# Block-causal attention with a gated convolutional unit: V rows of two tokens, masks by a minimum, products of 128x128, a searched order

## The chip, the cores and the metric

The kernel runs on one core of one Trainium2 chip. The metric is the device time of one execution in microseconds. Three runs of the kernel before have a median of 193.28 us (193.21 to 194.22). A profiled execution of it stands in the profile below, and all durations come from that one.

## What is computed

Eight batches of eight heads, 576 tokens, head width 64, all in float32. First attention whose mask is causal in blocks of 64 tokens, then a gated linear unit whose gate is a causal convolution of 5 taps along the tokens:

```python
scores = scale * np.matmul(q, k.transpose(0, 1, 3, 2))
mask = block_i >= block_j                      # blocks of 64 tokens
attn = softmax(np.where(mask, scores, -1e9))
x = np.matmul(attn, v)                         # (8, 8, 576, 64) -> (8, 576, 512)
gate = sigmoid(sum(conv_w[k] * xp[:, k:k + S, :] for k in range(5)))
out = (gate * (x @ w_val)) @ w_out             # (8, 576, 512)
```

## The kernel before, in words

The unit of work is a pair of heads; there are 32 pairs, four to a batch. The kernel is laid out as *steps*. Each step belongs to one engine and issues a handful of instructions there. A step's kind is a letter:

- **T** (33 steps, 16 products each, the first pair's in two of 8): `transposes` (L171) turns the fp16 casts of K and Q by identity products into PSUM; `evict_k` (L192, line L449) and `evict_q` (L458) copy them into the tile `kq`. **U** (8 steps): the same for the last 64 tokens of a batch (`evict_tail`, L480).
- **S** (three per pair): `scores` (L236), products of 64 rows; the two heads of a pair run in the two halves of the array. `exps` (L523) takes the exponential on ScalarE, 1024 columns a step, into the tile `pt`.
- masks: where a 128-row block of keys reaches beyond what a block of queries may see, the second half of its rows has to be zero. `zeros` (L280, line L542) writes zeros over rows 64 to 127 of two strips of `pt` per head, twice a pair, and `keep_last` (L274, line L530) copies one strip's rows 64 to 127 into `pd`. Each of these steps is on VectorE or GpSimd.
- **P** (one per pair, 30 products of 128x128 with 65 columns): `products` (L292) multiplies `pt` with the values `ve`, whose 65th column is one, so that the row sums come along. `sums` (L573) and `normal` (L583) divide on VectorE.
- **X** (10 products): `xt_steps` (L594) turns the result into `xt` (`evict_x`, L606). **G** (20 products of 64x64): `gate`, the convolution as products with diagonal matrices; `tanh` on ScalarE (L629).
- **V** (64 steps, 8 products of 128x64 with 288 columns): `val` multiplies with `w_val`, the two halves of the tokens side by side in the two column halves of the array; `gated` (L651) multiplies by the gate on VectorE into `gv`.
- **O** (19 steps, 16 products of 64x128 with 512 columns; the last tile in two steps of 256 columns): `out_tile` multiplies with `w_out`, `evict_out` (L674 on ScalarE, L676 on VectorE) copies 1024 columns to `ob`, and `store` (L684) sends them out.

All products go through one helper, so their line is L255. TensorE's shape of array differs by kind: T, U, S, X, O are 64x128, G is 64x64, V is 128x64, P is 128x128.

What sets the order: the table `ORDER` gives TensorE's steps, one letter each. `CHOICE` gives the engine of each step that could run on several. A planner (`plan`) walks through all steps with a table of costs and delays and puts every step at the place in its engine's instruction stream where it would start first; the instructions are then issued in that order, and on the chip each engine works its stream in order, with semaphores between them. Loads are steps of the SP queue in the order that `queue` lists. Where the planner sees TensorE without work before 60 us, it puts *fillers* into TensorE's stream: products of a zero tile `nought` with 128 columns, which keep the array busy.

Loads: K and Q of a pair are 256 KB each in runs of 1024 bytes (512 KB for two pairs from pair 8 on), through a ring of three buffers of two pairs. V comes in runs of 256 bytes, one token of one head to a partition row (`load_head` L138 for the first two batches, `load_v` L128 afterwards, 256 KB for 128 tokens of all eight heads), through a ring of five buffers. VectorE, GpSimd or ScalarE casts each into fp16 (L416).

Of the kernel before, what the change touches and what calls it, by code (L numbers as in the profile page):

```python
# [9 lines left out]
SUM_MAX = 60000.0  # L10

# [19 lines left out]
FROM, BUSY, FILL, FULL, NOUGHT = 1050, 9500.0, 60000.0, 4700, (108, 55)  # L31


WEIGH = {"PE": 0, "DVE": 83, "ACT": 69, "POOL": 127, "SP": 0}

ORDER = (
    "TTSUSSTSSSTPSSTcXSSSSPPXGPXTXUGVSSVGTGVSVSSVPSVTVPSSXTSVXSSSPGGXPUTGXTSVVGSSVVVS"
    "SVVVSTTPSSPSOXSPSXGXSTTGGSUPSSOXSPSSVVGTTVVSSSVVVVXSTTPSUPXSGGSXPSSOSXOSGGTSVVSS"
    "VVVSUTPPTSOSSVVVSXTPSSOXXGGSSOTSPPSSOXUGGTSVVXTSVVVVSSTPPSSOXSPXGGSXVVVSSTOTUVVS"
    "SSPPGGSTVVSXSVVVSSXPPSTOSSOSTOXXGGGSSTVVVVVVSSSPPPXSGGVVPXXOXGGGVVVVVVVVOOOfOO")  # L40

CHOICE = (
    "DDDADAPPPPDDDPDDDDDPAPDDDDPPPDDADPDADPPDDAAPADPDDDDPDPPDAAADDPPDDPPDADDDPDPPDAAD"
    "PPPADPPDDPPDDDDDPPPDPPPDDAAPPPPADDDDPPPPDPDADDDPDDPPDDPPPPADDPPDDPPPDDADDDDDDPPD"
    "DPDPDDPPDDDDPPDPDAADPPPDAADADPDPDPDDDDPPPPDPPAADDDPDPDDDDDDDAPPAAPDPDDADADPPDPPD"
    "DADPPPPDPDADDPPPAPPDDDPPPADPDDPDPPDDDPDDDDPPDDADPDDDDPPDDDPPDDPPDDDDDPDPPADPPPPA"
    "AAPAAPDPPDDDDPDDDDPPDADDDDDPPDDPPPPAPDADDPPDAAA")


class Step:  # L50


    def __init__(self, kind, key, engines, emit, needs, mode, banks, size, upper):
        self.kind, self.key, self.engines, self.emit = kind, key, engines, emit
        self.needs, self.mode, self.banks = list(needs), mode, banks
        self.size, self.upper = size, upper
# [6 lines left out]
class Planner:  # L63
# [6 lines left out]
    def add(self, kind, key, engines, emit, needs=(), mode=None, banks=0, size=None, upper=False):  # L70
# [33 lines left out]
    def plan(self):  # L104
        self.rank()
        free = dict(BEGIN)
        upper = {e: False for e in ENGINES}
        bank_free = [0.0] * 7 + [BUSY]
        mode, dma = None, 0.0
        lands = [0.0] * LANES  # L110
# [33 lines left out]
        def parts(s):  # L144
            rate = s.size[1]
            return s.size[0] / (256 if rate < 250 else 1024 if 300 < rate < 320 else 2048)
# [83 lines left out]
def kernel(  # L230
# [482 lines left out]
    def holds(s, *users):  # L713
        for u in users:
            u.held = s
# [429 lines left out]
```

## Time and profile before

| what | value |
|---|---|
| median of three runs | 193.28 us |
| the profiled execution, its own time | 193.37 us |
| its span, first to last instruction | 191.4 us |
| mean granted TensorE clock | 0.990 |
| instructions: matmul, VectorE, ScalarE, GpSimd | 3898, 335, 183, 161 |
| DMA packets, bytes | 64183, 41.02 MB |

The profile is one execution. Its span is about 2 us shorter than the execution's time, which holds what lies around the instructions. An engine's busy time is the time in which one of its instructions runs. Matmuls are pipelined: the record of one is as long as its passage through the array, several overlap, and the ends are modelled; so the price of a step is read from start to start, not from a mean duration. In a timeline row "x48" is a run of 48 like instructions, and the bracket holds the engine's idle time just before and what ended it. PEld is TensorE's load of the stationary operand, which runs ahead of the products.

### The profile page before, as it was taken

The page shows a single profiled execution, that of the slowest core. Times are in us where ns is not written, and L with a number is a line of the kernel's source. Part 1 is how long each engine was busy: PE and PEld are TensorE (multiplying, and loading weights), DVE is VectorE, ACT ScalarE, POOL GpSimd, SP SyncE. Part 2 cuts the span into 40 slices and gives each one's busy share as a digit, 9 for nine tenths or more (in the row PEclk, how much of TensorE's full clock was granted, in tenths as well). Part 3 has the DMA queues.
Part 4 walks back from the last instruction along what each step waited for, and adds up shares of the span by engine and source line. Part 5 has one row for each costly group of instructions (what it writes and reads, how often), then busy time and mean ns, then how long its engine had stood idle before and what let it go on. Part 6 is the DMA issues. An engine that isn't in the chain of part 4 may idle for free.

```text
span 191.4 us, 9072 instructions
## 1 busy us (share of the span) xinstructions
PE 176.8 (92%) x3898; PEld 130.3 (68%) x3898; DVE 137.6 (72%) x335; ACT 144.1 (75%) x183; POOL 69.4 (36%) x161
## 2 busy tenths in 40 slices
PE   7978999788999989999999999999999999999940
PEld 7766876566676747686686666777688568878430
DVE  5468775685978869897989756888977786876020
ACT  3587999497788969799789889688979877743430
POOL 5224451463674615535523546142716001100000
PEclk9999999999999999999999999999999999999996
DMA  5999999799869999969999799999981062004291
GB/s 152 264 284 306 216 235 340 190 272 198 255 154 263 242 295 262 255 157 322 333 225 270 190 317 288 238 279 281 270 268 47 37 207 92 3 3 113 93 305 56
DMA packets 64183, 41.02 MB, mean 214 GB/s; under 512 B 39301, under 2 KB 58757, under 8 KB 64138
## 3 DMA queue, kind: packets, MB, share of 16 engines
q1 hardware_dynamic: 63562, 39.87, 77.3%
q8 instruction: 32, 0.52, 1.2%
q10 hardware_dynamic: 576, 0.52, 0.9%
q14 instruction: 13, 0.11, 0.2%
HBM read 30.42 MB, written 9.44 MB: 208 GB/s over the span
## 4 chain that ended last, share of the span: by engine, by line
PE 65%; DMA 15%; DVE 9%; ACT 2%; issue 2%; SPq 2%; POOL 0%; ACTq 0%; DVEq 0%; POOLq 0%
PE ps L255 59%; DMA qraw<-in_q_dram 10%; PE ps L441 3%; DMA kraw<-in_k_dram 3%; PE ps L594 3%; DMA tail<-in_q_dram 2%; DVE gv L651 2%; DVE kq L449 1%; DVE w_out L416 1%; ACT kq L458 1%; DVE xn L583 1%; DVE qc L416 1%; SPq L386 1%; DVE kq L458 1%; DVE pd L530 1%
## 5 line engine op out<-in xcount | busy, mean ns | idle before, releaser
L523 ACT ACTIVATE pt<-ps 128x1024 f16<-128x1024 f32 x96 | 94.2, 1025 | 17.3 <-PE ps L255 13.8
L255 PE MATMUL ps<-xt,w_val 128*64 128x288 f16 x512 | 36.3, 288 | 0.0
L255 PE MATMUL ps<-kq 64*128 64x64 f16 (+4 forms) x448 | 33.2, 260 | 1.8 <-DVE kq L480 0.9
L255 PE MATMUL ps<-ve,pt 128*128 128x65 f16 x896 | 33.0, 193 | 1.1 <-issue 0.8
L255 PE MATMUL ps<-w_out,gv 64*128 64x512 f16 (+1 forms) x304 | 33.7, 365 | 0.0
L255 PEld LDWEIGHTS <-pt 128*128 128x128 f16 x896 | 30.1, 97 | 4.0 <-issue 2.1
L651 DVE SCALAR_TENSOR_TENSOR gv<-th,ps 128x288 f16<-128x288 f32 x64 | 27.2, 450 | 6.3 <-PE ps L255 5.3
L255 PEld LDWEIGHTS <-w_val 128*64 128x64 f16 x512 | 27.0, 110 | 5.1 <-issue 2.9
L583 DVE TENSOR_TENSOR xn<-ps,rinv 128x640 f16<-128x640 f32 x32 | 26.4, 824 | 1.1
L255 PEld LDWEIGHTS <-kq 64*128 64x128 f16 x448 | 16.0, 94 | 14.8 <-issue 5.6
L255 PE MATMUL ps<-xt,diag 64*64 64x288 f16 x640 | 23.4, 285 | 0.0
L255 PEld LDWEIGHTS <-gv 64*128 64x128 f16 x304 | 13.8, 94 | 13.2 <-issue 0.2
L629 ACT ACTIVATE th<-ps 128x576 f32<-128x576 f32 x32 | 20.1, 660 | 1.9 <-PE ps L255 1.7
L542 POOL MEMSET pt<- 64x256 f16 x41 | 13.2, 323 | 21.0 <-ACT pt L523 15.5
L255 PEld LDWEIGHTS <-diag 64*64 64x64 f16 x640 | 17.1, 106 | 2.5 <-issue 1.0
L416 POOL CAST qc<-qraw 128x512 f16<-128x512 f32 x22 | 13.6, 629 | 12.6 <-DMA qraw<-in_q_dram 12.1
L416 POOL CAST kc<-kraw 128x512 f16<-128x512 f32 x22 | 13.5, 630 | 12.7 <-DMA kraw<-in_k_dram 10.7
L449 DVE COPY kq<-ps 128x512 f16<-128x512 f16 x19 | 13.1, 690 | 6.9 <-PE ps L441 6.4
L676 DVE TENSOR_SCALAR ob<-ps 128x1024 f32<-128x1024 f32 (+1 forms) x12 | 13.1, 1090 | 3.9 <-PE ps L255 2.3
L255 PE MATMUL ps<-nought 128*128 128x128 f16 x132 | 11.8, 250 | 1.7 <-POOL nought L343 1.0
L674 ACT ACTIVATE ob<-ps 128x1024 f32<-128x1024 f32 (+1 forms) x9 | 8.0, 885 | 6.7 <-PE ps L255 6.7
L573 DVE RECIPROCAL rinv<-ps 128x10 f32<-128x10 f32 x32 | 6.9, 216 | 8.0 <-PE ps L255 7.7
(67 smaller groups left out, 207.4 us busy)
## 6 DMA issues: line engine op xcount, KB each, us to landing
kraw<-in_k_dram SPq DMA_DIRECT2D x12, 512.0 KB, 5.2
qraw<-in_q_dram SPq DMA_DIRECT2D x12, 512.0 KB, 6.5
vraw<-in_v_dram SPq DMA_DIRECT2D x24, 256.0 KB, 6.4
out_dram<-ob SPq DMA_DIRECT2D x11, 512.0 KB, 4.0
kraw<-in_k_dram SPq DMA_DIRECT2D x8, 256.0 KB, 4.3
vraw<-in_v_dram SPq DMA_DIRECT2D x16, 128.0 KB, 5.2
qraw<-in_q_dram SPq DMA_DIRECT2D x7, 256.0 KB, 5.3
out_dram<-ob SPq DMA_DIRECT2D x4, 384.0 KB, 5.7
```

Of the source, the lines that this page charges most:

```text
L255: nc.tensor.matmul(out=out, lhsT=lhsT, rhs=rhs, start=start, stop=stop, skip_group_check=True)
L416: copier(s.engine)(out=out, in_=in_)
L441: nc.tensor.transpose(out=o, in_=c16[name][rows, t, :, :], identity=ident16[rows, rows])
L449: copier(s.engine)(out=kqs[:, p % NT, K0:K0 + 512].rearrange("p (r s t) -> p r s t", r=2, t=4), in_=ps16[:, i:i + 2, 256:512].rearrange("p ...
L523: nc.scalar.activation(out=heads(p)[:, :, 512 * c:512 * c + 512], in_=ps[:, i:i + 2, :], func=AF.Exp, bias=0.0, scale=0.125)
L542: setter(s.engine).memset(seg[:, :, :, 0:64], 0.0)
L573: nc.vector.reciprocal(out=rinv[:, p, :, :].rearrange("p e (c x) -> p e c x", x=1), in_=o[:, :, :, 64:65])
L583: nc.vector.tensor_tensor(out=xns[p % NX][:, :, :, :].rearrange("p c e d -> p e c d"), in0=o[:, :, :, 0:64], in1=ri.to_broadcast([128, 2, ...
L629: nc.scalar.activation(out=ths[at % NTH][:, 0:n, :, :].rearrange("p n r x -> p (n r) x"), in_=ps[:, i:i + 2 * n, 0:HALF], func=AF.Tanh, bi ...
L651: nc.vector.scalar_tensor_tensor(out=gv[:, 2 * g + r, s0:s0 + HALF], in0=ths[at % NTH][:, n, r, :], scalar=1.0, in1=ps[:, va.group[0], 0:H ...
L674: nc.scalar.activation(out=o, in_=x, func=AF.Copy, bias=0.0, scale=0.5)
L676: nc.vector.tensor_scalar(out=o, in0=x, scalar1=0.5, scalar2=None, op0=ALU.mult)
```

## The change

Seven edits go together.

- **V in rows of two tokens.** A partition row now holds two neighbouring tokens of a head, so a run is 512 bytes. `load_v` fetches 256 tokens of four heads in 256 KB, `load_head` as before 128 KB. The cast into `ve` becomes four (or two times two) pieces of 64 partitions (`spread`). Since key rows are now ordered by pairs of tokens, the masked rows are 32 to 63 and 96 to 127 of a 128-row block; the writes of K into `kq`, the last 64 keys and the duplicate of them follow the same order.
- **Masks.** On VectorE `zeros` and `keep_last` are a minimum over all 128 partitions with a per-partition number, 0 or 65504 (`keep`); on GpSimd they are two instructions of 32 partitions each. Eight small memsets fill `keep` at the start.
- **V as products of 128x128.** A step is 4 products of 288 columns; its left operand is the 128 columns of a group of channels or, for the second half of the tokens, the same with the 64-wide halves exchanged, for which `w_val` gets a copy of 64 columns per group.
- **O as products of 128x128.** A tile is two steps of 4 products of 512 columns, each with one bank and an eviction of 512 columns of its own; later tiles are stored in halves.
- **Loads of one pair.** K and Q are always loaded for one pair, 256 KB, through a ring of six; the table `LOADS` sets the order of all loads.
- **The planner's numbers**: delays between engines, a price for each block of 128 products on TensorE, DMA delays; and with them new tables `ORDER`, `LOADS` and `CHOICE`. TensorE's table has 137 neighbours of different array shape where there were 129.
- **Fillers** have 512 columns, are priced 430 ns before 4.7 us and 215 ns after, and stop at 25 us. There are 33 of them, 17 ahead of the first transposition; before there were 132, 30 of them ahead of it.

At the start of the SP queue, before; `kraw`, `qraw` and `vraw` are landing buffers by number; the first pair's K is ahead of these rows, its Q goes through ScalarE's queue, and the first row is the tail of K:

```order
L339 DMA tail320_96<-in_k_dram 64x1x256 x2
L333 DMA kraw0_77<-in_k_dram 128x2x256
L333 DMA qraw0_80<-in_q_dram 128x2x256
L406 DMA vtail320_100<-in_v_dram 64x8x64
L397 DMA vraw0_83<-in_v_dram 128x4x64 x2
L736 DMA conv_nat_65<-in_moe_conv_w_dram 5x512
L333 DMA kraw1_78<-in_k_dram 128x2x256
```

The same place now:

```order
L366 DMA tail320_100<-in_k_dram 64x1x256 x2
L362 DMA qraw2_85<-in_q_dram 128x2x256
L362 DMA qraw1_84<-in_q_dram 128x2x256
L362 DMA kraw1_78<-in_k_dram 128x2x256
L362 DMA kraw2_79<-in_k_dram 128x2x256
L793 DMA conv_nat_65<-in_moe_conv_w_dram 5x512
L423 DMA vraw0_89<-in_v_dram 128x2x128
L362 DMA kraw3_80<-in_k_dram 128x2x256
```

K and Q of the second and third pair have moved ahead of the first V, and V's rows are 128 elements long where they were 64.

On VectorE, around the copy of the convolution's weights `convT`, before; `kc`, `qc`, `ve` are fp16 casts, `pt` and `pd` the masked exponentials, `xt` the transposed result:

```order
L416 CAST ve0_104<-vraw1_84 128x8x64
L530 COPY pd1_112<-pt1_108 64x128
L542 MEMSET pt1_108 64x2x2x32
L449 COPY kq0_106<-ps_133 128x512
L416 COPY kq0_106<-kq0_106 128x64
L739 COPY convT_66<-ps_133 128x20
L606 COPY xt0_118<-ps_133 128x2x5x64
```

The same stretch now:

```order
L497 COPY kq0_109<-ps_136 128x512
L455 COPY kq0_109<-kq0_109 128x2x32
L455 CAST kc163_95<-kraw3_80 128x2x4x64
L796 COPY convT_66<-ps_136 128x20
L600 TENSOR_SCALAR pt0_110<-pt0_110,keep0_134 128x2x2x64 x2
L438 CAST ve0_107<-vraw0_89 64x4x64 x2
L455 CAST qc160_96<-qraw4_87 128x2x4x64
L488 COPY kq0_109<-ps_136 128x512
```

A pair's two masks are now one `TENSOR_SCALAR` each on 128 rows (before, a `COPY` and a `MEMSET` on 64), V's cast is in pieces of 64 rows, and more casts and copies of K and Q for later pairs stand ahead of the first `xt`, which is further back.

The diff, cut to its core:

```diff
-    "PE": {"PE": 0, "DVE": 265, "ACT": 250, "POOL": 240, "SP": 60},
-    "DVE": {"PE": 53, "DVE": 35, "ACT": 45, "POOL": 105, "SP": 27},
-    "ACT": {"PE": 53, "DVE": 40, "ACT": 20, "POOL": 115, "SP": 25},
-    "POOL": {"PE": 52, "DVE": 40, "ACT": 45, "POOL": 60, "SP": 30},
+    "PE": {"PE": 0, "DVE": 105, "ACT": 90, "POOL": 240, "SP": 60},
+    "DVE": {"PE": 228, "DVE": 35, "ACT": 45, "POOL": 105, "SP": 27},
+    "ACT": {"PE": 228, "DVE": 40, "ACT": 20, "POOL": 115, "SP": 25},
+    "POOL": {"PE": 228, "DVE": 40, "ACT": 45, "POOL": 60, "SP": 30},
...
+PRODUCTS = {"T": 16, "U": 8, "S": 14 / 3, "P": 30, "X": 10, "G": 20, "V": 4, "O": 4, "c": 4, "f": 1}
+BLOCK, EARLIER, BUSY_L, FREE_L = 128, 95, 4400.0, 2700.0
...
-SETUP, SEEN, LANES, SLOTS, SINGLE = 1000, 1400, 8, 2048, 8
-FROM, BUSY, FILL, FULL, NOUGHT = 1050, 9500.0, 60000.0, 4700, (108, 55)
...
+SETUP, SEEN, LANES, SLOTS, SLOW, STORED = 1000, 1700, 8, 2048, 1.05, 700
+BEFORE = (0.0, 0.0, 3950.0, 4400.0, 5900.0, 5900.0, 6100.0, 6300.0)
+FROM, FILL, FULL, NOUGHT = 1050, 25000.0, 4700, (430, 215)
...
-    "TTSUSSTSSSTPSSTcXSSSSPPXGPXTXUGVSSVGTGVSVSSVPSVTVPSSXTSVXSSSPGGXPUTGXTSVVGSSVVVS"
+    "TTUSSSTTScSSSSTSTPSSSXPGPXPSXGXUGTSVSVSTGSSVSVPTSVVSXSPVGSXSTPVSPXUGGSXTSVVSSTVV"
...
+    7, 1, 0, 6, 5, 3, 10, 8, 11, 4, 23, 2, 22, 16, 9, 18, 13, 14, 12, 17, 33, 28, 21,
...
-    w_val_sb = ring(1, [128, 4, 512], fp16, "w_val")[0]
+    w_val_sb = ring(1, [128, 4, 4, 192], fp16, "w_val")[0]
...
-    NRAW, NVR, NC, NT, NPT, NX, NXT, NTH, NOB = 3, 5, 4, 8, 4, 3, 3, 8, 4
+    NRAW, NVR, NC, NT, NPT, NX, NXT, NTH, NOB = 6, 3, 4, 8, 4, 3, 3, 7, 4
-    raws = {n: ring(NRAW, [128, 4, 4, 64], fp32, n + "raw") for n in ("k", "q")}
+    raws = {n: ring(NRAW, [128, 2, 4, 64], fp32, n + "raw") for n in ("k", "q")}
-    vraws = ring(NVR, [128, 8, 64], fp32, "vraw")
+    vraws = ring(NVR, [128, 8, 128], fp32, "vraw")
...
-    def load_v(b, c):
-        t = vraws[(4 * b + c) % NVR]
+                    lambda _: load_runs(nc.sync, src, t, p), 262144, RUN[1024],
+                    before(p - NRAW, "c" + name), 500)
+    def load_v(p, c):
+        b, j = divmod(p, PPB)
+        t = vraws[p // 2 % NVR][:, c:8:2, :]
         def emit(_):
-            nc.sync.dma_start(out=t[:, :, :],
-                              in_=v[b, :, 128 * c:128 * c + 128, :].rearrange("h p d -> p h d"))
-        n = 4 * b + c - NVR
-        return load(PPB * b - 3.5, emit, 262144, RUN[256], [chunks[n]] if n >= 0 else [], 620)
+            nc.sync.dma_start(out=t, in_=v[b, 2 * j:2 * j + 4, 256 * c:256 * c + 256, :].rearrange(
+                "h (p u) d -> p h (u d)", u=2))
...
-        t = vraws[p % NVR][:, 4 * e:4 * e + 4, :]
+        t = vraw(p)[:, 2 * e:2 * e + 2, :]
         def emit(_):
             nc.sync.dma_start(out=t, in_=v[b, 2 * j + e, 0:512, :].rearrange(
-                "(c p) d -> p c d", p=128))
-        n = p - NVR
-        return load(p - 3.5, emit, 131072, RUN[256], [chunks[n]] if n >= 0 else [], 520)
+                "(c p u) d -> p c (u d)", p=128, u=2))
...
+        def emit(s):
+            for out, in_ in todo:
+                copier(s.engine)(out=out, in_=in_)
+        return add("", key, engines, emit, needs, upper={"POOL": on, "DVE": on})
...
     def keep_last(p):
         def emit(s):
-            copier(s.engine)(
-                out=pds[p % NPT][64:128, 0:128].rearrange("p (e x) -> p e x", e=2),
-                in_=heads(p)[64:128, :, 960:1024])
+            to = pds[p % NPT][:, 0:128].rearrange("p (e x) -> p e x", e=2)
+            if s.engine == "POOL":
+                for x in (32, 96):
+                    nc.gpsimd.tensor_copy(out=to[x:x + 32], in_=heads(p)[x:x + 32, :, 960:1024])
+            else:
+                nc.vector.tensor_scalar(out=to, in0=heads(p)[:, :, 960:1024],
+                                        scalar1=keep[:, 0:1], scalar2=None, op0=ALU.min)
         return emit
     def zeros(p, first):
         def emit(s):
             if first:
-                seg = heads(p)[64:128, :, 0:1024].rearrange("p e (s x) -> p e s x", x=512)
+                at, step = 0, 512
             else:
-                seg = heads(p)[64:128, :, 960:1344].rearrange("p e (s x) -> p e s x", x=192)
-            setter(s.engine).memset(seg[:, :, :, 0:64], 0.0)
+                at, step = 960, 192
+            if s.engine == "POOL":
+                seg = halves(p)[:, :, at // 2:at // 2 + step].rearrange("p e (s x) -> p e s x", s=2)
+                for x in (32, 96):
+                    nc.gpsimd.memset(seg[x:x + 32, :, :, 0:32], 0)
+            else:
+                seg = heads(p)[:, :, at:at + 2 * step].rearrange("p e (s x) -> p e s x", s=2)
+                seg = seg[:, :, :, 0:64]
+                nc.vector.tensor_scalar(out=seg, in0=seg, scalar1=keep[:, 1:2], scalar2=None,
+                                        op0=ALU.min)
         return emit
...
     def val(b, g, r):
         def emit(s):
-            n0 = 128 * g + 64 * r
+            s0 = PAD + HALF * r
             for fc in range(4):
-                for c in range(2):
-                    s0 = PAD + HALF * c
-                    mm(out=ps[64 * c:64 * c + 64, s.group[0], 0:HALF],
-                       lhsT=w_val_sb[:, fc, n0:n0 + 64], rhs=xts[b % NXT][:, fc, s0:s0 + HALF],
-                       start=(fc == 0), stop=(fc == 3))
+                mm(out=ps[:, s.group[0], 0:HALF], lhsT=w_val_sb[:, fc, g, 64 * r:64 * r + 128],
+                   rhs=xts[b % NXT][:, fc, s0:s0 + HALF], start=(fc == 0), stop=(fc == 3))
...
+    def out_tile(i, es):
+        def emit(s):
+            for n, e in enumerate(es):
+                for g in range(4):
+                    mm(out=ps[:, s.group[0] + n, :], lhsT=gv[:, g, e, 128 * i:128 * i + 128],
+                       rhs=w_out_sb[:, 2 * g + e, :], start=(g == 0), stop=(g == 3))
...
+        "mask": memsets(0, {"DVE": 1100}, [(keep[x:x + 32, n:n + 1], (0.0, BIG)[(n + x // 32) % 2])
+                                           for x in (0, 32, 64, 96) for n in range(2)]),
...
-                o = add("O", p, {"PE": 870 if last else 1727}, out_tile(i, cols),
-                        need + lo + ([sf] if last else []), "A", 2)
+            done = []
+            for e in range(2):
+                o = add("O", p, {"PE": 870}, out_tile(i, (e,)),
+                        [pairs[x]["gv"][e] for _, _, c in parts for x in range(PPB * c, PPB * c + 4)]
+                        + lo + ([sf] if last else []), "C", 1)
...
+                    done.append(add("", p, {"ACT": 600, "DVE": 690},
+                                    evict_out(n, o, (e,), slice(0, 512)), [o] + old))
+                    holds(o, done[-1])
...
+                mid = (lo_ + hi_) // 2
+                for x, x0, x1 in (("ACT", lo_, mid), ("SP", mid, hi_)):
+                    stores[n].append(add("", p, {x: 440}, store(n, c, x0, x1, (e,)), evs,
+                                         size=((x1 - x0) * 2048, RUN[0])))
...
-                    mm(out=ps[:, s.group[0], 0:128], lhsT=nought[:, :], rhs=nought[:, :])
+                    mm(out=ps[:, s.group[0], :].rearrange("p (o x) -> p o x", o=4), lhsT=nought[:, :],
+                       rhs=nought[:, :].rearrange("p (o x) -> p o x", o=1).to_broadcast([128, 4, 128]))
```

More of the change, by code (lines that the diff above doesn't have):

```diff
@@ L106, in plan @@
         free = dict(BEGIN)
-        upper = {e: False for e in ENGINES}
-        bank_free = [0.0] * 7 + [BUSY]
+        upper = {e: 0 for e in ENGINES}
+        bank_free = [0.0] * 8
         mode, dma = None, 0.0
-        lands = [0.0] * LANES
+        count, edge, seen = 0.0, EARLIER, -1e9
+        lands = list(BEFORE)
         sent = []
@@ L904 @@
                      for c in range(UNIT) if HALF * c < x1 and HALF * c + HALF > x0]
-            need = [s for _, _, c in parts for x in range(PPB * c, PPB * c + 4)
-                    for s in pairs[x]["gv"]]
             old = [s for s in stores[n - NOB]] if n >= NOB else batches[0]["lent"].get(n, [])
@@ L948, in queue @@
                 yield from weights[2:4]
-        for p in range(8, NP, 2):
+        for p in range(8, NP):
             b = p // PPB
@@ L954, in queue @@
             if p % PPB == 0:
-                yield from (batches[b]["lv"], *batches[b]["lc"])
-    last = None
-    for s in queue():
+                yield batches[b]["lv"]
+            yield from pairs[p].get("lv", [])
+    last, listed = None, list(queue())
+    assert sorted(LOADS) == list(range(len(listed)))
+    for n in LOADS:
+        s = listed[n]
         s.load = True
```

259 lines of the change are left out of this document (141 added, 118 removed), and 7 rows, old and new, of the table LOADS.

## The prediction

> **What bounds the kernel now.** I read the page first: the engines, TensorE's busy tenths, and the shares of the chain that ended last.
>
> ```profile
> PE 176.8 (92%) x3898; PEld 130.3 (68%) x3898; DVE 137.6 (72%) x335; ACT 144.1 (75%) x183; POOL 69.4 (36%) x161
> PE   7978999788999989999999999999999999999940
> PE 65%; DMA 15%; DVE 9%; ACT 2%; issue 2%; SPq 2%; POOL 0%; ACTq 0%; DVEq 0%; POOLq 0%
> ```
>
> TensorE is the chain for two thirds of the span, with DMA behind it; its tenths dip only in the first 17 slices (4.8 us each) and at the end. A busy TensorE need not be at its peak, so I next took a stretch of its timeline in which nothing waits, where one step's start to the next one's is its price.
>
> ```profile
> 157.47 0.28 PE L441 MATMUL ps<-ident,kc 64*128 64x64 f16 x8
> ...
> 157.82 3.13 PE L255 MATMUL ps<-xt,w_val 128*64 128x288 f16 x48
> 160.89 0.86 PE L255 MATMUL ps<-kq 64*128 64x128 f16 x14
> 161.68 0.60 PE L255 MATMUL ps<-ve,pt 128*128 128x65 f16 x14
> ...
> 164.52 0.29 PE L594 MATMUL ps<-perm,xn 64*128 64x64 f16 x8
> ...
> 164.67 0.38 PE L255 MATMUL ps<-kq 64*128 64x128 f16 x6
> 164.99 1.42 PE L255 MATMUL ps<-xt,diag 64*64 64x288 f16 x40
> 166.34 1.17 PE L255 MATMUL ps<-xt,w_val 128*64 128x288 f16 x16
> ...
> 170.73 2.04 PE L255 MATMUL ps<-xt,diag 64*64 64x288 f16 x60
> 172.70 4.11 PE L255 MATMUL ps<-xt,w_val 128*64 128x288 f16 x64
> 176.74 5.35 PE L255 MATMUL ps<-w_out,gv 64*128 64x512 f16 x48
> 182.03 0.19 PE L255 MATMUL ps<-ones,allr 128*1 128x1 f32 x2
> 182.15 1.92 PE L255 MATMUL ps<-w_out,gv 64*128 64x256 f16 x32
> ```
>
> Two G and what follows take 166.34 - 164.99 = 1.35 us, three take 172.70 - 170.73 = 1.97: a G is 0.62, and 0.1 is left for the change of array shape behind it. Eight V take 4.04, six 3.07: a V is 0.49. Three O take 5.29, so 1.73 each. With 0.1 taken off for each change of shape, three P (161.68 to 164.52) are 0.91 each, a pair's S (160.89 to 161.68) 0.69, T 0.25, X 0.15. A pair is then 0.25 + 0.69 + 0.91 + 0.15 + 0.62 + 2 x 0.49 = 3.60 us, 32 pairs 115.2. Eighteen tiles of O are 31.1; the U steps and small ones I put at 1.4, an estimate at half a T each. Sum 147.7. 129 changes of shape at 0.1 add 12.9: **160.6 us** of work that no wait explains.
>
> TensorE's stream runs from 1.01 (below) to 182.15 + 1.92 = 184.07, so 183.1 us. The remaining 22.5 are fillers and waits.
>
> ```profile
> L255 PE MATMUL ps<-nought 128*128 128x128 f16 x132 | 11.8, 250 | 1.7 <-POOL nought L343 1.0
> ...
> 1.01 3.38 PE L255 MATMUL ps<-nought 128*128 128x128 f16 x30 [1.01 <-POOL nought L343]
> 4.42 0.40 PE L441 MATMUL ps<-ident,kc 64*128 64x64 f16 x8
> ...
> 5.72 1.28 PE L255 MATMUL ps<-nought 128*128 128x128 f16 x12
> 6.93 0.39 PE L255 MATMUL ps<-kq 64*128 64x512 f16 x2
> ...
> 7.37 1.12 PE L255 MATMUL ps<-nought 128*128 128x128 f16 x17
> 8.42 0.64 PE L255 MATMUL ps<-kq 64*128 64x448 f16 x12
> ```
>
> Fillers take 11.8; so **10.7 us are waits**. The load rows of TensorE show the long ones:
>
> ```profile
> 35.02 0.17 PEld L441 LDWEIGHTS <-kc 64*128 64x128 f16 x8 [1.09 <-POOL kc L416]
> 35.67 0.17 PEld L441 LDWEIGHTS <-qc 64*128 64x128 f16 x8 [0.48 <-DVE qc L416]
> ...
> 39.23 0.17 PEld L441 LDWEIGHTS <-kc 64*128 64x128 f16 x7 [0.78 <-issue]
> ...
> 45.63 0.24 PEld L255 LDWEIGHTS <-pt 128*128 128x128 f16 x6 [0.94 <-issue]
> 68.87 0.42 PEld L255 LDWEIGHTS <-kq 64*128 64x128 f16 x12 [1.04 <-DVE kq L480]
> ```
>
> Two are casts behind late K and Q. The one at 45.63 falls in the middle of a P, whose operands are all there, with "issue" beside it: TensorE had no instructions. 16 KB of them come in at a time, 32 times:
>
> ```profile
> q8 instruction: 32, 0.52, 1.2%
> ```
>
> **The change, part by part.** *V and O as 128x128.* 64 V steps of 4 products with 288 columns replace 8 products that ran two at a time: 0.49 before, 4 x 0.12 = 0.48 now, by the same columns. O: 4 products of 512 columns twice, against eight pairs of 512: 1.73 again. TensorE gains nothing here; it issues 256 + 160 products fewer. The changes of shape go from 129 to 137: +0.8.
>
> *Instructions.* 3898 becomes about 3380 products with fewer fillers, so some 28 blocks instead of 32. The wait of 0.94 goes where a dense stretch no longer meets a block's edge; I count 0.9, bounds 0 and 2. The Trainium skill, "Runtime: NRT & Kernel Launch", section Instruction fetch mechanics, says that crossing a block is mostly hidden because the engine dispatches more slowly than blocks come in. By that the saving would be 0 and the sum 0.9 higher. The row at 45.63 does not agree with it: 0.94 us without an instruction in the middle of a step.
>
> *Fillers.* A 128-column filler costs 3.38 / 30, some 0.107 us, at the start and 1.05 / 17 = 0.06 from about 6.6 us on, when the clock had risen. One of 512 columns costs four times that: 0.43 cold, 0.22 to 0.24 warm. Seventeen stand ahead of the first transposition. If the clock rises at 6.6 again, 13 run cold (5.6 us) and 4 warm (0.9): the first transposition comes at 7.5 instead of 4.42. That is 3.1 us of late start, though more of K and Q will have landed by then. The other 16 are 3.6. Together 10.1 against 11.8: -1.7. Bounds: all 17 cold, 8.3 us (+0.8); a rise at 4.5 us, -1.2.
>
> *Loads.* V in runs of 512 bytes:
>
> ```profile
> kraw<-in_k_dram SPq DMA_DIRECT2D x8, 256.0 KB, 4.3
> vraw<-in_v_dram SPq DMA_DIRECT2D x24, 256.0 KB, 6.4
> ```
>
> The same 256 KB lands in 4.3 us in runs of 1024 bytes and in 6.4 in runs of 256. With 512 it lies between; I take 5.4. That brings the first pairs' K and Q forward, which moreover now stand ahead of V in the queue, and TensorE starts 3 us later. The SP queue issues some 26 loads more at about 0.45 us, off the path. So of the 10.7 us of waits the casts behind late loads (1.09 + 0.48 + 0.78) and the small ones before 25 us (about 3) go.
>
> *VectorE.*
>
> ```profile
> L542 DVE MEMSET pt<- 64x128 uint32 x23 | 3.7, 165 | 1.8 <-ACT pt L523 1.3
> L530 DVE COPY pd<-pt 64x128 f16<-64x128 f16 x15 | 3.5, 232 | 2.3 <-ACT pt L523 2.0
> L449 DVE COPY kq<-ps 128x512 f16<-128x512 f16 x19 | 13.1, 690 | 6.9 <-PE ps L441 6.4
> L676 DVE TENSOR_SCALAR ob<-ps 128x1024 f32<-128x1024 f32 x10 | 12.2, 1223 | 2.5 <-PE ps L255 0.9 <-ACT pt L523 0.7 <-issue 0.7
> L676 DVE TENSOR_SCALAR ob<-ps 128x256 f32<-128x256 f32 x2 | 0.8, 425 | 1.4 <-PE ps L255 1.4
> ...
> 10.35 0.21 DVE L416 COPY kq<-kq 128x64 f16<-128x64 f16 x1
> ...
> 17.43 0.29 POOL L530 COPY pd<-pt 64x128 f16<-64x128 f16 x1
> ...
> 17.43 0.58 DVE L416 COPY kq<-kq 128x64 f16<-128x64 f16 x1
> ```
>
> The order gives it 47 masks where it had 38. No row shows a minimum. The nearest is the small copy within SBUF: 0.21 us, or 0.58 when a copy on GpSimd starts at the same moment (17.43). I take 0.3, nearer to the free one, since GpSimd is idle 64% of the span: 47 x 0.3 = 14.1 against 7.2, +7. An eviction of 512 columns lies between 425 and 1223 ns at 0.69; 20 of them and two small ones are 14.7 against 13.1. Five more K copies (0.69) add 3.5, small casts 2. VectorE goes from 137.6 to about 152 us of some 183, 83%: not the bound, but with less slack. I charge 1 us of new waits (bounds 0 and 13, rivals).
>
> *The sum.* Waits: 10.7 - 2.3 - 3 - 0.9 + 1 = 4.5; the bounds are 1 and 10.7. 193.37 (the profiled run; 0.09 over the median) + 0.8 - 1.7 - 6.2 = 186.3. The order is new throughout, so the wait at 68.87 (1.04 for a copy of the tail) need not recur; with it gone 185.2, and that is the forecast: 185. The end, 191.4 - 184.07 = 7.3 us of evictions and stores, stays: the last step is split alike.
>
> **The rivals.** *1. VectorE's masks become the wait* (slower). Every P stands behind the last mask of its pair, in the same queue as the copies that T, X and V need. If a mask takes 0.58 where it took 0.17 and TensorE has nothing ahead of P to cover it, each pair loses 0.41 for each exposed mask: with one in every pair 32 x 0.41 = 13 us, 198. It decides from 20 exposed masks on (8.2 us). For it: the row at 17.43, and VectorE's fuller queue. Against: the chain has VectorE at 9% only. The Trainium skill, "SBUF — State Buffer", section Who interferes with whom, states such a rule: a tensor_scalar in a two-port mode and a GpSimd instruction exclude each other, the later one blocking fully. The row at 17.43 agrees (0.58 against 0.21). By that rule, with GpSimd busy for some half of the new span, half the masks would take 0.58 and VectorE 4 us more in all.
>
> *2. The waits only change place* (no change). They came from the loads' and casts' order as a whole, and a new order has as many: 10.7 stay, 193.37 + 0.8 - 1.7 = 192.5. For it: a third of the 10.7 has no named cause. Against: from 84 us on TensorE waits almost nowhere.
>
> *3. The 512-byte runs land no sooner*: the change does not do what it says, the 2.3 us stay, 187.5.
>
> *4. Nearly all waits go*, 1.5 us left: 182.
>
> **How the numbers follow.** Forecast 0.55, rival 4 0.18, rival 3 0.10, rival 2 0.09, rival 1 0.08. The range, 180.5 to 191, leaves out rivals 1 and 2 and takes in the filler bounds (-1.2, +0.8). About 0.5% (1 us) is what a measurement of this kernel tells from no change: faster is the first three, 0.83; same, most of rival 2, 0.08; slower 0.09.
>
> **What would show it.** Right: V at 0.48 and O at 0.86 a step from start to start; the first transposition near 7.5 us; fillers about 10 us; no "issue" wait near 1 us inside a P; waits of TensorE after 25 us under 4 us. Wrong: masks on VectorE over 0.4 us with TensorE's P waiting on them; waits for casts of K or Q as before; or a first transposition at 8 us and TensorE short of work behind it.

## The result, and the profile after

The changed kernel takes 191.92 us (median; 191.16 to 192.7) where the kernel before took 194.35 beside it: a ratio of 0.992 (95% interval 0.9894 to 0.9945), 0.8% faster. The forecast was 185, some 4%. The profiled execution has a span of 190.0 us and a time of 191.91; before it was 191.4 and 193.37. Some executions of a kernel are over 1.5% longer than its fastest; ratios here and below leave them out, medians don't.

The page of the changed kernel; its tenths are of 4.75 us each:

```profile
PE 176.3 (93%) x3383; PEld 117.7 (62%) x3383; DVE 150.1 (79%) x375; ACT 145.2 (76%) x195; POOL 96.4 (51%) x242
...
PE   7997898997999999999999999999999999999960
...
DVE  6499998998998998788887979989698916866520
...
q8 instruction: 28, 0.46, 1.0%
...
PE 69%; DMA 11%; DVE 11%; ACT 3%; issue 2%; POOL 1%; SPq 0%; POOLq 0%; DVEq 0%; ACTq 0%
...
vraw<-in_v_dram SPq DMA_DIRECT2D x24, 256.0 KB, 5.5
```

In the chain DMA has gone from 15% to 11% and VectorE risen from 9% to 11%; VectorE is busy 150.1 us instead of 137.6. TensorE's tenths still dip in the first part of the span, and nowhere behind it. Its timeline at the start and near the end:

```profile
1.01 5.82 PE L284 MATMUL ps<-nought 128*128 128x512 f16 x17 [1.01 <-POOL nought L370]
6.76 0.29 PE L480 MATMUL ps<-ident,kc 64*128 64x64 f16 x8
...
173.13 3.60 PE L284 MATMUL ps<-xt,w_val 128*128 128x288 f16 x28
176.57 1.03 PE L284 MATMUL ps<-w_out,gv 128*128 128x512 f16 x4
...
177.92 2.75 PE L284 MATMUL ps<-w_out,gv 128*128 128x512 f16 x12
180.61 0.19 PE L284 MATMUL ps<-ones,allr 128*1 128x1 f32 x2
180.73 2.76 PE L284 MATMUL ps<-w_out,gv 128*128 128x512 f16 x12
```

Seven V take 176.57 - 173.13 = 3.44 us. V and O now have the same shape of array, so nothing changes behind them, and a V is 0.49, as before. Three O take 2.69 with one change, so 0.86. The stream ends at 180.73 + 2.76 = 183.49: 182.5 us, of which 160.6 + 0.8 are work and 10.1 fillers, as forecast:

```profile
L284 PE MATMUL ps<-nought 128*128 128x512 f16 x33 | 10.1, 452 | 1.5 <-POOL nought L370 1.0 <-ACT pt L570 0.5
```

That leaves **11.0 us of waits**, where the prediction had 10.7 before and wrote 4.5 for now (its own terms add up to 5.5, see below). The balance against before: fillers -1.7, changes of shape +0.8, waits +0.3, the end behind the last product 6.5 instead of 7.3; together -1.4, and that is the difference of the two profiled executions. The expected gain went back into waits. Where they are now, the windows say. Busy time by engine from 10 to 50 us (columns: window, its length, PE, PEld, DVE, ACT, POOL, each with its instructions, then the clock, the share of the DMA engines and GB/s), before:

```profile
10.00:20.00 10.00, 8.89 (x196) 7.12 (x195) 7.07 (x21) 8.19 (x10) 3.75 (x10) 1.00 1.09 290
20.00:30.00 10.00, 10.00 (x266) 7.66 (x263) 7.29 (x18) 9.79 (x17) 4.76 (x10) 1.00 0.93 242
30.00:40.00 10.00, 8.10 (x176) 5.53 (x174) 6.87 (x18) 7.40 (x10) 3.01 (x6) 1.00 0.88 232
40.00:50.00 10.00, 9.03 (x238) 6.75 (x238) 7.59 (x20) 8.17 (x12) 5.51 (x13) 1.00 1.08 253
```

and in the changed kernel:

```profile
10.00:20.00 10.00, 8.51 (x153) 4.80 (x149) 9.04 (x26) 8.85 (x11) 5.47 (x15) 1.00 1.13 302
20.00:30.00 10.00, 9.27 (x238) 7.06 (x240) 9.79 (x25) 9.87 (x16) 6.76 (x17) 1.00 1.05 285
30.00:40.00 10.00, 8.76 (x188) 6.38 (x188) 8.82 (x22) 8.38 (x11) 8.47 (x22) 1.00 1.02 296
40.00:50.00 10.00, 8.28 (x219) 6.21 (x212) 8.93 (x19) 7.41 (x12) 8.36 (x19) 1.00 0.81 214
```

VectorE, 28.8 of 40 us before, is busy for 36.6: it has little room left in the stretch in which TensorE waits. ScalarE is full from 20 to 30 us in both. What went is the wait for loads. The waits of the kernel before in that stretch that a DMA ended (us in total, times, longest):

```profile
POOL kc L416 <- DMA kraw<-in_k_dram: 3.9, 2, 2.4
...
DVE qc L416 <- DMA qraw<-in_q_dram: 2.7, 2, 1.4
...
POOL qc L416 <- DMA qraw<-in_q_dram: 1.8, 3, 1.1
```

In the changed kernel's answer for the same stretch, which lists waits from 0.2 us on, no DMA ends one. VectorE's and TensorE's waits there look like this; VectorE first:

```profile
17.36 0.27 DVE L600 TENSOR_SCALAR pt<-pt,keep 128x256 f16<-128x256 f16 x1
...
30.96 0.68 DVE L582 TENSOR_SCALAR pd<-pt,keep 128x128 f16<-128x128 f16 x1 [0.63 <-POOL pt L596]
31.56 0.68 DVE L488 COPY kq<-ps 128x512 f16<-128x512 f16 x1
32.16 0.41 DVE L497 COPY kq<-ps 128x512 f16<-128x512 f16 x1
...
43.56 0.69 DVE L582 TENSOR_SCALAR pd<-pt,keep 128x128 f16<-128x128 f16 x1 [0.81 <-POOL pt L596]
...
44.35 0.66 DVE L600 TENSOR_SCALAR pt<-pt,keep 128x256 f16<-128x256 f16 x1
```

and TensorE:

```profile
32.62 0.65 PE L284 MATMUL ps<-xt,w_val 128*128 128x288 f16 x4 [0.81 <-DVE kq L497]
...
43.58 0.33 PE L284 MATMUL ps<-ve,pt 128*128 128x65 f16 x5
45.07 0.45 PE L284 MATMUL ps<-ve,pt 128*128 128x65 f16 x9 [1.17 <-DVE pt L600]
```

At 30.33 the copy into `pd` stands at the head of VectorE's queue and waits 0.63 us for GpSimd's zeros; the copies of K and Q behind it are late, and at 31.8 TensorE waits 0.81 for the PSUM bank that they hold. At 42.75 the same wait, 0.81, is followed by a copy of 0.69 and a mask of 0.66, and a P stands for 1.17. By the code the copy into `pd` needs only the exponentials. But the strips that GpSimd clears and the strip that VectorE copies lie interleaved in `pt`, head by head, and the built program orders the two as if they overlapped.

### The profile page after: what moved, and what is told of

Read it like the earlier page. It is cut to its first block, busy times and chain, and to the rows that moved or that the text cites. A ratio compares the mean times of both kernels' runs of the same rounds, so it can differ in the third digit from the quotient of the medians.

```text
span 190.0 us, 8230 instructions
## 1 busy us (share of the span) xinstructions
PE 176.3 (93%) x3383; PEld 117.7 (62%) x3383; DVE 150.1 (79%) x375; ACT 145.2 (76%) x195; POOL 96.4 (51%) x242
## 4 chain that ended last, share of the span: by engine, by line
PE 69%; DMA 11%; DVE 11%; ACT 3%; issue 2%; POOL 1%; SPq 0%; POOLq 0%; DVEq 0%; ACTq 0%
PE ps L284 63%; DMA vraw<-in_v_dram 5%; PE ps L480 3%; DVE xn L642 3%; DMA tail<-in_q_dram 2%; PE ps L653 2%; DMA qraw<-in_q_dram 2%; DMA ob<-in_moe_w_out_dram 2%; ACT pt L570 2%; DVE ve L438 1%; DVE kq L488 1%; DVE pt L600 1%; ACT th L688 1%; DVE qc L455 1%; POOL pt L596 1%
## 5 line engine op out<-in xcount | busy, mean ns | idle before, releaser
L284 PE MATMUL ps<-xt,w_val 128*128 128x288 f16 x256 | 37.8, 287 | 1.1 <-DVE kq L497 0.8
L284 PE MATMUL ps<-w_out,gv 128*128 128x512 f16 x144 | 36.3, 380 | 0.0
L596 POOL MEMSET pt<- 32x128 uint32 x70 | 15.4, 221 | 30.5 <-ACT pt L570 16.3
L284 PEld LDWEIGHTS <-w_val 128*128 128x128 f16 x256 | 22.9, 98 | 10.0 <-issue 2.8
L642 DVE TENSOR_TENSOR xn<-ps,rinv 128x640 f16<-128x640 f32 x32 | 26.4, 824 | 1.0
L438 POOL CAST ve<-vraw 64x512 f16<-64x512 f32 (+1 forms) x47 | 25.4, 542 | 2.4
L284 PEld LDWEIGHTS <-kq 64*128 64x128 f16 x448 | 16.1, 94 | 16.3 <-issue 10.1
L488 DVE COPY kq<-ps 128x512 f16<-128x512 f16 x24 | 16.4, 688 | 4.5 <-PE ps L480 3.5
L284 PEld LDWEIGHTS <-gv 128*128 128x128 f16 x144 | 12.5, 98 | 11.2 <-issue 0.6
L730 DVE TENSOR_SCALAR ob<-ps 128x512 f32<-128x512 f32 (+1 forms) x22 | 14.5, 661 | 5.7 <-PE ps L284 2.9
L728 ACT ACTIVATE ob<-ps 128x512 f32<-128x512 f32 (+1 forms) x16 | 9.2, 573 | 10.7 <-PE ps L284 10.6
L580 POOL COPY pd<-pt 32x128 f16<-32x128 f16 x28 | 8.6, 306 | 12.6 <-ACT pt L570 11.6
```

Of the source, the lines that this page charges most:

```text
L284: nc.tensor.matmul(out=out, lhsT=lhsT, rhs=rhs, start=start, stop=stop, skip_group_check=True)
L438: copier(s.engine)(out=out, in_=in_)
L488: copier(s.engine)(out=kqs[:, p % NT, K0:K0 + 512].rearrange("p (r x s w) -> p r x s w", r=2, s=32, w=2), in_=ps16[:, i:i + 2, 256:512].re ...
L580: nc.gpsimd.tensor_copy(out=to[x:x + 32], in_=heads(p)[x:x + 32, :, 960:1024])
L596: nc.gpsimd.memset(seg[x:x + 32, :, :, 0:32], 0)
L642: nc.vector.tensor_tensor(out=xns[p % NX][:, :, :, :].rearrange("p c e d -> p e c d"), in0=o[:, :, :, 0:64], in1=ri.to_broadcast([128, 2, ...
```

## The experiments

**Theory A**: the waits of the loads became waits of VectorE's queue: it is full there, masks take more of it, and its head stands still for GpSimd's zeros. **Theory B**: TensorE still waits for what the loads bring. **Theory C**: the late first transposition is a loss of its own. Ratios are to the kernel before; the changed kernel has 0.992.

### The order stop, the fillers, all masks, V's loads

```diff
+APART = (4, 5, 7, 11, 14, 20)
...
+                    if first and p in APART:
+                        for e in range(2):
+                            nc.gpsimd.memset(seg[x:x + 32, e, :, 0:32], 0)
...
+                for e in range(2) if p in APART else (slice(0, 2),):
+                    nc.vector.tensor_scalar(out=to[:, e], in0=heads(p)[:, e, 960:1024],
```

> The changed kernel; in six pairs (4, 5, 7, 11, 14, 20) the copy of the strip into pd on VectorE is made head by head and GpSimd's zeros of the first strips too, so that the copy no longer stands behind those zeros; same results, 6 instructions more on VectorE and 12 more on GpSimd. Theory A (the waits of the loads have become waits of VectorE's queue, whose head stands still for GpSimd's zeros at 30.3, 34.6 and 42.7 us): these three stops (0.63, 0.28, 0.81 us) go, and with them most of TensorE's waits at 31.43 (0.88), 35.03 (0.45) and 43.58 (1.35): 1.5 to 2.5 us faster than the changed kernel, 0.979 to 0.984 of before. Theory B (TensorE still waits for what the loads bring): no more than 0.3 us, 0.991.

Measured: 189.91 us, 0.9793 (0.9755 to 0.9831), 1.3% below the changed kernel. The P at 43 us waits 0.52 where it waited 1.17:

```profile
43.50 0.33 PE L285 MATMUL ps<-ve,pt 128*128 128x65 f16 x5
44.34 0.45 PE L285 MATMUL ps<-ve,pt 128*128 128x65 f16 x9 [0.52 <-DVE pt L606]
```

This is as A has it. In its trace the first transposition came 0.85 us later than in the changed kernel's; 2.3 us are won between 31 and 82 us, and from 102 us to the end every step of TensorE starts 1.47 to 1.48 us sooner, without another change. What is won or lost by then is carried to the end one for one.

```diff
-                for _ in range(int(spare / NOUGHT[s.start > FULL])):
+                for _ in range(int(spare / NOUGHT[s.start > FULL + 1000])):
```

> The changed kernel with 8 fillers instead of 17 ahead of the first transposition (the gap was divided by the price of a warm filler, 215 ns, though ten of them took 427). The first transposition should come at about 4.9 us instead of 6.76. Theory C (the late start is a loss of its own that is carried to the end): 1 to 1.8 us faster than the changed kernel, about 0.985 of before. Theory A (behind the start VectorE's casts and copies set the pace, 9.0 of 10 us busy from 10 to 20): at most 0.4 us.

Measured: 191.18 us, 0.986 (0.9811 to 0.9909). The start:

```profile
1.01 3.59 PE L284 MATMUL ps<-nought 128*128 128x512 f16 x8 [1.01 <-POOL nought L370]
5.03 0.39 PE L480 MATMUL ps<-ident,kc 64*128 64x64 f16 x8 [0.43 <-DVE kc L455]
```

The first transposition is 1.73 us sooner, the first U (which waits for the tail's cast) 0.97, and 0.97 to 1.0 stays to the end of the stream. Theory C holds at 1 us in the trace; in the times the interval reaches from 0.1 to 1.1% below 0.992. Both edits together:

> The changed kernel with both edits: 8 fillers ahead of the first transposition, and the copy into pd and GpSimd's zeros head by head in the six pairs. Same results. If the two losses add up (each shifts all that comes behind it): about 1 us under the kernel with the mask edit alone, 0.974 of before. If the earlier start is eaten by VectorE's queue in the first 50 us: 0.979.

Measured: 189.0 us, 0.9815 (0.9774 to 0.9855). By the times this is not told apart from the mask edit alone. In its trace the stream ends at 181.0 instead of 182.0; a stop of 0.74 us in a G at 25 us, with "issue" beside it, had taken part of the gain (see instruction blocks below).

With both emitters left empty (`keep_last` and `zeros` return at once):

> The changed kernel with no mask written at all: neither the zeros nor the copy into pd, on either engine (so scores of later tokens are not masked). VectorE loses 47 instructions (16.1 us), GpSimd 98 (24 us). Theory A: TensorE's waits between 25 and 100 us go for the most part, 4 to 6 us faster than the changed kernel, 0.961 to 0.971 of before. Theory B: under 1 us, 0.987 to 0.992.

Measured: 187.28 us, 0.9663 (0.9618 to 0.9709): the masks cost the changed kernel 2.6%, 5 us. The same edit on the kernel before:

> The kernel before with no mask written (neither zeros nor the copy into pd, so scores of later tokens are not masked). Theory A (in the kernel before VectorE had room, 7.2 of 10 us busy from 10 to 50, and the loads bound): 0 to 1.5 us faster, 0.992 to 1. If masks cost as much there as in the changed kernel, where leaving them out took 2.6% off: 4 to 5 us, 0.974 to 0.979.

Measured: 193.63 us, 1.0032 (0.9996 to 1.0068): nothing. (Its profiled execution, 191.75, is its fastest, and in that one the stops at 35 us shrink as well; the median doesn't follow.) Masks were free before and cost 5 us now. That is what A asks. VectorE's share is not the whole of it: without masks it is as busy from 10 to 50 us, 36.0 of 40, but TensorE gets 37.3 us of work done there instead of 34.8.

The loads of V, first with buffers set to zero (`load_v` and `load_head` issue nothing), then for the later pairs alone:

> The changed kernel without the loads of V's first 512 tokens (the landing buffers are set to zero once, on GpSimd, so the values are not the input's); casts and all else stay. A third of the loaded bytes go, and K and Q land earlier. Theory A (VectorE's queue): no more than 1 us, 0.987 to 0.992 of before. Theory B (loads): 3 to 5 us faster than the changed kernel, 0.966 to 0.977.

Measured: 194.26 us, 1.0076 (1.0029 to 1.0123), slower than either theory has it. In its profile an X stops for 1.80 us at 26.4 with "issue" as its releaser, so this run doesn't judge the loads.

```diff
+            if p >= 6:
+                return
             nc.sync.dma_start(out=t, in_=v[b, 2 * j + e, 0:512, :].rearrange(
```

> The changed kernel without the loads of V from the seventh pair on (the landing buffers keep the first six pairs' V, so the values are not the input's); nothing is added on any engine, unlike the run that set the buffers to zero. Theory A (VectorE's queue): at most 0.5 us faster than the changed kernel, 0.989 to 0.994 of before. Theory B (loads bind from 25 to 50 us): 2 to 4 us, 0.971 to 0.982.

> The kernel before without the loads of V from the sixth pair on (the landing buffers keep the first five pairs' V, so the values are not the input's). If its waits from 33 to 45 us were waits for late K and Q, as the prediction had it: 2 to 3 us faster than before, 0.985 to 0.990. If VectorE's queue set the pace there as well: under 0.5 us, 0.997 to 1.

Measured: the changed kernel so cut 193.07 us, 1.0005 (0.9972 to 1.0038), no faster than the whole one, and why it is 0.8% slower stays open. Its trace has TensorE's waits of 0.81 and 1.17 as they were. For V's later loads theory B falls. K, Q, the tails and the weights were not tried, and the chain that ended last runs through DMA from 25 to 43 us in the changed kernel (V, `w_out`, a tail of Q). The kernel before so cut 194.96 us, 0.9968 (0.9922 to 1.0014), between the two expectations. Its trace gains 1.6 us around 35 us and 1.2 at 67, where the prediction had put waits for late K, Q and tails, and loses 1.64 again in a G (the row at 84.50 below). As a time it is inconclusive. One of the three waits that the prediction put on late loads, 0.78 at 39.23, did not move: it stands at 38.51 in this run, again 0.78 with "issue" beside it, while the two others went.

### V's loads undone, masks undone

```diff
-            nc.sync.dma_start(out=t, in_=v[b, 2 * j:2 * j + 4, 256 * c:256 * c + 256, :].rearrange(
-                "h (p u) d -> p h (u d)", u=2))
+            for u in range(2):
+                nc.sync.dma_start(out=t[:, :, 64 * u:64 * u + 64],
...
```

> The changed kernel with V's loads in runs of 256 bytes again: the same rows and landing buffers, each load in two halves of one token each, 40 issues more on the SP queue. Same results. Theory A (VectorE's queue binds and the loads have slack): V lands later, yet the time stays within 1 us of the changed kernel, 0.990 to 0.997 of before. Theory B (loads): 2 to 4 us slower, 1.002 to 1.013.

Measured: 201.38 us, 1.0437 (1.0374 to 1.0501). Theory A's number here was wrong by 9 us, and B's too small. This run changes two things, so the next one keeps 512-byte runs and doubles only the issues:

```diff
+            for h in (0, 2):
+                nc.sync.dma_start(out=t[:, h:h + 2, :],
...
```

> The changed kernel with each load of V in two halves, by heads or by token blocks: runs of 512 bytes stay, and the SP queue issues the same 40 transfers more as in the run with 256-byte runs, which took 201.4 us. Same results. If the 9 us lost there came from the shorter runs: close to the changed kernel, 0.990 to 1.000 of before. If they came from the issues (each holds the SP queue about half a microsecond, and K and Q stand behind them): most of it is lost here too, 1.025 to 1.045.

Measured: 198.38 us, 1.0323 (1.0278 to 1.0368). Of the 5.2% over the changed kernel 4.0 are the 40 issues, 7.8 us by the ratios (the two profiled executions differ by 6.0), and about 1.1 the shorter runs (each of the two ratios is known to some 0.5%). The SP queue in this run (issue, its duration):

```profile
11.54 0.62 SPq L362 DMA_DIRECT2D kraw<-in_k_dram  x1
12.20 2.78 SPq L426 DMA_DIRECT2D vraw<-in_v_dram  x4
15.03 0.56 SPq L366 DMA_DIRECT2D tail<-in_k_dram  x1
15.63 1.06 SPq L426 DMA_DIRECT2D vraw<-in_v_dram  x2
```

One issue follows the other without a gap at 0.5 to 0.7 us each, and K and Q stand behind V's. Once issued, K lands in 4.1 us where it took 5.2, which points at the issue coming late. The changed kernel's loads are just in time: fewer bytes of V give nothing, 40 issues more take 7.8 us. Part of this may be the clock, whose granted share (the number after POOL's) fell in this execution around a stop of 2.15 us at 44 us:

```profile
40.00:50.00 10.00, 7.09 (x137) 5.14 (x138) 6.10 (x15) 4.86 (x8) 6.86 (x17) 0.75 0.91 262
```

How much of the 7.8 us that is was not measured; the execution with a mean clock of 0.995 still took 196.88 us.

```diff
-                nc.vector.tensor_scalar(out=seg, in0=seg, scalar1=keep[:, 1:2], scalar2=None,
-                                        op0=ALU.min)
+                for x in (32, 96):
+                    nc.vector.memset(seg[x:x + 32, :, :, 0:32], 0)
```

> The changed kernel with VectorE's masks made as GpSimd makes them: two writes of zeros, or two copies, of 32 rows each, instead of one minimum over 128 rows. Same results. If the minimum is dear because GpSimd holds it up (0.66 us at 44.35 against 0.27 free) and the pieces are not held up: VectorE's masks 16.1 us now, 12 to 13 then, and 0.5 to 1.5 us faster than the changed kernel, 0.984 to 0.989 of before. If two pieces cost as much as one minimum: no difference, 0.992.

Measured: 197.58 us, 1.0212 (1.0178 to 1.0247), 2.9% slower: both expectations were on the wrong side. The masks by groups in the changed kernel, and then with pieces:

```profile
L600 DVE TENSOR_SCALAR pt<-pt,keep 128x256 f16<-128x256 f16 x29 | 10.5, 369 | 0.6 <-ACT pt L570 0.3
...
L582 DVE TENSOR_SCALAR pd<-pt,keep 128x128 f16<-128x128 f16 x18 | 5.6, 312 | 4.1 <-POOL pt L596 2.8 <-ACT pt L570 1.3
```

```profile
L600 DVE MEMSET pt<- 32x128 uint32 x58 | 9.6, 165 | 6.0 <-ACT pt L570 1.3 <-DMA qraw<-in_q_dram 0.5 <-POOL kc L455 0.3
L583 DVE COPY pd<-pt 32x128 f16<-32x128 f16 x36 | 9.1, 252 | 3.9 <-ACT pt L570 1.6 <-POOL pt L596 1.4
```

A write of zeros over 32 rows takes 165 ns, as one over 64 rows did before: for this write the rows are free and the instruction is paid. VectorE's masks rise from 16.1 to 18.7 us, and idle time ahead of the zeros from 0.6 to 6.0. So with the order of V's new rows, which splits each mask in two strips of 32 rows, the minimum is the cheaper way. The run is 2.9% slower, 5.6 us, more than the 2.6 us of busy time; what the rest is was not tried apart.

### Instruction blocks

A stop with "issue" beside it is one in which TensorE waited for nothing that the profile shows. The one in the middle of a P came back at the same product when the kernel before ran without its masks, and without V's later loads:

```profile
44.97 0.36 PE L255 MATMUL ps<-ve,pt 128*128 128x65 f16 x6 [1.02 <-issue]
```

```profile
45.29 0.36 PE L255 MATMUL ps<-ve,pt 128*128 128x65 f16 x6 [1.20 <-issue]
84.50 0.93 PE L255 MATMUL ps<-xt,diag 64*64 64x288 f16 x24 [1.45 <-issue]
```

Counted along TensorE's stream from 0, the stops in P are at product 862 and that in G at 1758. Two others are at product 350: the G at 25 us of the run with both edits (0.74 us) and the X at 26.4 of the one without V's loads (1.80). All of them are 94 past a multiple of 128. With 32 blocks for 3898 products and 28 for 3383, a block holds some 121 or 122, close to that distance. That is why the stops are put down to instruction blocks.

The changed kernel's profile has no such stop. In two runs its products were split, so that there are more of them:

```diff
+                for x in (0, HALF // 2):
+                    mm(out=ps[:, s.group[0], x:x + HALF // 2], lhsT=w_val_sb[:, fc, g, 64 * r:64 * r + 128],
...
```

> The changed kernel with each of V's products split in two of 144 columns: the same columns, 256 products more (3639 instead of 3383), that is 2 instruction blocks of 16 KB more. Same results. If instruction blocks can stop TensorE where products are dense (0.94 us inside a P in the kernel before, 1.45 us inside a G in the run of it without V's loads): stops of 1 to 2 us with nothing else waited for come back, 1.5 to 4 us slower than the changed kernel, 1.000 to 1.012 of before, and a wider spread of the runs. If blocks always come in time: 0 to 1 us, 0.992 to 0.997.

Measured: 192.6 us, 0.9981 (0.9935 to 1.0027), between the two expectations, and no stop over 0.5 us (one of 0.49 at product 350). Contrary to its expectation the results of V are not the kernel's; instructions and columns are. V is not where products are dense, so the gate's were split:

```diff
-                    for r, c in ((0, 0), (1, 1), (0, 1), (1, 0)):
+                for at in (0, HALF // 2):
+                    for j in range(5):
+                        for r, c in ((0, 0), (1, 1), (0, 1), (1, 0)):
...
```

> The changed kernel with each product of the gate's convolution split in two of 144 columns: the same columns, 640 products more, where they were already dense (31 ns each). Same results. The split of V's products by the run before brought no stop, but V's are 0.12 us each and so not dense. If instruction blocks stop TensorE where products are dense: 5 blocks more are fetched, and stops of 0.4 to 1.5 us without a releaser appear behind or inside G, 3 to 10 us slower in all, 1.008 to 1.045 of before. If not: a G rises by what its loads of the stationary operand take, evenly, below 0.2 us each or 6 us in all, and no stop appears.

Measured: 197.94 us, 1.0315 (1.0263 to 1.0367). A single G takes 757 ns from start to next start where it took 741, so the products themselves cost next to nothing. Stops appear in the profiled execution:

```profile
25.39 0.48 PE L284 MATMUL ps<-ve,pt 128*128 128x65 f16 x10 [0.60 <-issue]
29.66 0.20 PE L480 MATMUL ps<-ident,kc 64*128 64x64 f16 x1 [0.82 <-issue]
71.40 0.24 PE L284 MATMUL ps<-ve,pt 128*128 128x65 f16 x1 [3.39 <-issue]
143.57 0.76 PE L284 MATMUL ps<-xt,diag 64*64 64x144 f16 x35 [0.89 <-issue]
...
183.46 0.66 PE L284 MATMUL ps<-xt,diag 64*64 64x144 f16 x29 [1.16 <-issue]
```

Five blocks more (33 instead of 28) and five stops of 6.9 us in all with nothing else waited for, at products 350, 478, 1373, 3036 and 3932: 92 to 94 past a multiple of 128 again. This execution took 202.6 us, more than the others, and its 3.39 us stop is not to be taken for theirs; from 70 to 80 us, behind it, the granted clock is 0.66. By the ratios, which leave it out, the loss is 4%, 7.7 us, of which 0.016 us more for each of 32 G is 0.5. That stops make up the rest there too is likely but not shown, since only this execution has a profile. The Trainium skill, "Runtime: NRT & Kernel Launch", section Instruction fetch mechanics, has the crossing of a block mostly hidden; the traces agree for most blocks, and for those named here they do not, by 0.6 to 3.39 us each.

### The best version

The mask's pieces head by head in twelve pairs, and 8 fillers:

> The changed kernel with 8 fillers ahead of the first transposition, and with the mask's pieces head by head in all twelve pairs in which VectorE makes the copy into pd and GpSimd the first zeros (instead of six). Same results. If GpSimd's waits for VectorE's copy (2.2 us in three places) reach TensorE as well: 0.5 to 1 us under the kernel with both edits, 0.976 to 0.979 of before. If not: the same, 0.981.

Measured: 188.17 us, 0.9737 (0.9697 to 0.9778): by its median the fastest of the kernels that compute the whole reference, 1.8% under the changed kernel; its interval overlaps those of the two runs with six pairs. Its stream of products ends 1.9 us ahead of that with both edits in six pairs. It is 0.75 ahead at 30 us, most of it because the stop at 25 us isn't there, and a further 1.15 comes in steps from 65 us on, which fits the six further pairs.

## Why the prediction was wrong

- **V, O, shapes, fillers.** Right: V 0.49 (0.48 forecast), O 0.86, fillers 10.1 us. TensorE gains nothing there.
- **The start.** Forecast 7.5 us, measured 6.76; the trace has the clock rise at 5.05 us, before at 6.67. That the late start would be lost was left open; 1 us of it is carried to the end.
- **Instructions.** Right: the 0.94 us stop inside a P is gone. With other products such stops come back, at the same distance in the stream.
- **Loads.** V lands in 5.5 us (5.4 forecast; 4.9 to 5.8 in the other profiles with the same loads), and casts no longer wait for a DMA from 10 to 50 us. The mechanism was right. K and Q did not land sooner: 5.2 us each, where 256 KB of them took 4.3 and 5.3 before. That more SP issues lie "off the path" has no margin: 40 further ones cost 7.8 us.
- **VectorE's masks.** 0.37 and 0.31 us (0.3 forecast), busy 150.1 us (152). At 44.35 a mask took 0.66 while GpSimd cast, at 17.36 it took 0.27, as rival 1 had it. Of the 47, 35 take 0.24 to 0.30 us; the other 12, beside which a GpSimd cast runs for 0.37 us or more, take 0.37 to 0.69. The Trainium skill, "SBUF — State Buffer", section Who interferes with whom, has that lock for a tensor_scalar in a two-port mode, and the trace agrees; the writes of zeros in pieces stayed at 165 ns each.
- **The step that failed**: "I charge 1 us of new waits". By leaving the masks out, on VectorE and GpSimd, they measure 5 us (2.6%). VectorE was judged by its share of the span, 83%, "not the bound, but with less slack". But of the 12.5 us put on it, 7.8 fell into the 40 us where the removed waits lay, and took it from 72% to 91% there. About half of the 5 us is the order stop (1.3%), which no row of before showed on VectorE. The other half, the masks' own time in the two queues, is argued and was not tried apart.
- **The sum.** 10.7 - 2.3 - 3 - 0.9 + 1 is 5.5, not 4.5: the charge of 1 us never entered the forecast. With it the sum gives 186.2 instead of 185.2, still 5.7 short of the profiled 191.91.
- **The waits that were to go** (6.2 us): the named long ones are gone, and as many came. The 3 us of small ones before 25 us did not go as far as the windows show: TensorE is without a product for 1.5 us from 10 to 20 us, where it was for 1.1. And 0.78 of the loads' 2.3 us was no wait for a load (above). Rival 2, 192.5 with a chance of 0.09, is what happened, by part of rival 1's mechanism. The end is 0.8 us shorter, which was not forecast.

Open: of the 11.0 us of waits some 6 remain even without masks. V's later loads are not their cause. What the first pairs' way through the exponentials, VectorE and the banks costs was not tried apart.

## What to carry to other kernels

When a wait is taken away, ask into which ten microseconds the new work on each other engine falls, not what share of the span it has: here VectorE had 72% in the stretch and over the whole span alike, and most of its new work fell into the stretch. When two engines use interleaved strips of one tile, the program can order them one behind the other though they touch different columns; an instruction at the head of an engine's queue then holds up all behind it. On a path this tight a microsecond won or lost early is mostly carried to the end, and stops of dense products at instruction blocks belong in the sum.

## What was not expected of the hardware

- The clock does not rise at a fixed moment. The traces have it at 5.05 us in the changed kernel and at 6.78 in that of the mask edit. The same 17 fillers took 5.82 us and 6.67, so the first transposition came at 6.76 and 7.62:

```profile
1.01 6.67 PE L285 MATMUL ps<-nought 128*128 128x512 f16 x17 [1.01 <-POOL nought L371]
7.62 0.29 PE L481 MATMUL ps<-ident,kc 64*128 64x64 f16 x8
```

- The stop at an instruction block varies widely for one and the same product: at product 350 from nothing (the changed kernel) over 0.49, 0.60 and 0.74 to 1.80 us; the longest at any was 3.39.
- A write of zeros on VectorE is paid by the instruction: 165 ns for 32 rows as for 64.
